# First block's hidden product in whole float32, and another order of the start, in an attention and feed-forward kernel on one NeuronCore

## The chip, the cores and the metric

The kernel runs on one core of a Trainium2 chip. The core has five engines, each with its own instruction queue that is worked off in order: TensorE (PE, matrix products; its weight loads are listed apart as PEld), VectorE (DVE), ScalarE (ACT), GpSimd (POOL) and SyncE (SP). SP and POOL issue the DMA transfers here. The metric is the device time of one execution in microseconds (us).

## The reference, cut to what matters

Inputs are `q`, `k`, `v` of 8 batches, 8 heads, 576 tokens, 64 channels in float32, and two weight matrices in float64, `w_in` (512 x 2048) and `w_out` (2048 x 512).

```
q_d, k_d, v_d = means over 4 neighbouring tokens                 # 144 tokens
out = repeat(softmax(q_d k_d^T / 8) v_d, 4)  +  softmax(q k^T / 8, only |i-j| < 4) v
x = out as (8*576) x 512                                         # tokens x (head, channel)
h = x @ w_in
P = a0 + a1 h + a2 h^2 + a3 h^3 ;  Q = 1 + |b0||h| + |b1| h^2
result = (P / (Q + 1e-6)) @ w_out
```

## The kernel before, in words

The work is written as tasks with an engine, an estimated length, tiles read and written, and sometimes a due time. A planner (`Plan.run`, L117) lists them: on each engine, of the tasks whose inputs are ready, the one with the earliest latest start goes first. The result is a fixed order for each engine; on the chip only the order holds, and each instruction waits for its own inputs. `due_h(n)` (L645) gives the due time of step n of the feed-forward part: `H0` + 8.0 n in the first block, then 6.2 a step.

Attention goes by batches, two heads (a pair) at a time, four pairs a batch. For a pair, `load_qk` and `load_vw` bring the inputs; `scores` (L391) puts a mask into two PSUM banks with two bf16 products (L397) and adds local scores in windows of 64 x 64 (L406); `pool_qk` and `scores_pooled` (L423) do the pooled ones; `softmax_local` and `softmax_pooled` take maxima on DVE and exponentials on ACT (L453, L479); `normalize` scales on DVE; `turned` transposes on PE (L527, L534) and copies back on ACT (L540, L550); `weighted` (L556) multiplies by v (L576, L565), and `put_x` (L608) adds the parts into x on DVE. The first batch (L798 on) runs by itself, two pairs at a time, over all eight banks. Later batches share two banks and run beside the feed-forward part.

The feed-forward part takes blocks of 512 tokens (and two blocks of 256), 16 steps each. Step n: `h_part` (L665) multiplies x by 128 columns of `w_in` into one of two banks; `middle` (L691) reads the bank with four activations (L689) and makes the quotient with further work on ACT and DVE; `o_part` (L724), two steps later, multiplies by 128 rows of `w_out` into four banks (L741). After its last step a block is stored. Products run in fp32r, which keeps fewer bits than float32, so each operand is split into a high part (rounded by a cast) and a low part (the rest), and a product is three: high x high, low x high, high x low. `split_x` (L649) splits x, one ACT cast and one DVE subtraction for each of four 128-column parts.

The weights come as float64. `weights` (L305) loads a chunk of 512 KB into a spot that several chunks share, scales the upper words on ACT (L325), joins the two words into float32 bits on DVE (L328, L331; tile `wb`), casts these to the high part on ACT (L340; `wh`) and subtracts on DVE (L343; `wl`, in the place of `wb`). There are 16 chunks of each matrix. They are wanted in the order in which the first block's steps need them.

Of the kernel before, what the change touches and what calls it, by code (L numbers as in the profile page):

```python
# [9 lines left out]
F32 = mybir.dt.float32  # L10
BF16 = mybir.dt.bfloat16
# [19 lines left out]
NW = 10  # L31
# [136 lines left out]
def attention_moe(  # L168
# [12 lines left out]
    nc = tc.nc  # L181
# [3 lines left out]
    add = plan.add  # L185
# [5 lines left out]
    def put(name, shape, dtype, at=None):  # L191
        nonlocal top
        offset = top if at is None else at
        n = 2 if dtype == BF16 else 4
        for d in shape[1:]:
            n *= d
        if at is None:
            top = -(-(offset + n) // 32) * 32
        ap = nc.alloc_sbuf_tensor_at(name, shape, dtype, offset=offset).ap()
        room = Room(ap, (("S", k) for k in range(offset // 32, -(-(offset + n) // 32))))  # L200
        room.at = offset
        room.size = n
        return room
# [10 lines left out]
    high, low, bits = [], [], [[], []]  # L214
# [9 lines left out]
    xs, xsf = [], []  # L224
# [5 lines left out]
    gb = [put(f"gb{i}", [P, DM], F32, g.at) for i, g in enumerate(gt)]  # L230
    ident = put("ident", [P, P], F32)
    identb = put("identb", [P, P], BF16)
    maskb = put("maskb", [P, NW // 2 * D], BF16)
    cf = put("cf", [P, 8], F32)
    scales = put("scales", [P, 16], F32)
    nms = [put(f"nm{i}", [P, 16], F32) for i in range(4)]
# [54 lines left out]
    add("DVE", 0.1, lambda: nc.vector.memset(scales.ap[:, :NW], scale), (), (scales,))  # L291
    add("DVE", 0.1, lambda: nc.vector.memset(scales.ap[:, NW:], scale / 16.0), (), (scales,))
    add("DVE", 0.2, lambda: nc.vector.tensor_copy(out=identb.ap, in_=ident.ap), (ident,), (identb,))
    add("SP", 0.4, lambda: nc.sync.dma_start(out=maskb.ap, in_=mask), (), (maskb,))

    def setup_coef():
        add("SP", 0.1, lambda: nc.sync.dma_start(out=cf.ap[:, :6], in_=coef), (), (cf,), due=30.0)
# [4 lines left out]
        )  # L302


    def weights(w, f, spot):  # L305
        st = spot.ap.rearrange("p (c f two) -> p c f two", two=2, c=NCC)
        hi, lo, word = high[w][f], low[w][f], bits[w][f]

        def load():
            if w == 0:  # L310
                nc.sync.dma_start(
                    out=st.rearrange("p c f two -> p c (f two)"),
                    in_=w_in[:, 2 * f * P : 2 * (f + 1) * P].rearrange("(c p) f -> p c f", p=P),
                )
            else:
                nc.sync.dma_start(
                    out=st.rearrange("p c f two -> p (c f two)"), in_=w_out[f * P : (f + 1) * P, :]
                )

# [15 lines left out]

        add("SP", 1.4, load, (), (spot,))
        add("ACT", 0.58, scaled, (spot,), (spot,))
        add("DVE", 0.335, upper, (spot,), (lo,))
        add("DVE", 0.6, lower, (spot, lo), (lo,))
        add("ACT", 0.53, lambda: nc.scalar.copy(out=hi.ap, in_=word.ap.bitcast(F32)), (lo,), (hi,))  # L340
        add(
            "DVE", 0.6,
            lambda: nc.vector.tensor_tensor(  # L343
                out=lo.ap, in0=word.ap.bitcast(F32), in1=hi.ap.bitcast(F32), op=ALU.subtract
            ),
            (lo, hi), (lo,),
        )


# [7 lines left out]
        def pos(self, j):  # L357
            return j ^ self.odd

    def load_qk(c):  # L360
        s, b, i = c.slot, c.b, c.i
        add("SP", 1.6, lambda: nc.sync.dma_start(out=s.qk.ap, in_=qk[b, i]), (), (s.qk,))

    def load_vw(c):
        s, b, i = c.slot, c.b, c.i
        add("SP", 0.9, lambda: nc.sync.dma_start(out=s.vw.ap, in_=vw[b, i]), (), (s.vw,))

    def load_pooled(c):

# [21 lines left out]
    def scores(c, bk):  # L391

        s = c.slot

        def issue():
            for j in range(2):
                nc.tensor.matmul(  # L397
                    bk[j].ap[:, : NW // 2 * D], lhsT=identb.ap, rhs=maskb.ap,
                    start=True, stop=False, skip_group_check=True,
                )  # L400
            for w in range(0, NW, 2):
                for j in range(2):
                    js = slice(j * D, (j + 1) * D)
                    for g in range(2):
                        o = (w + g) * WQ
                        nc.tensor.matmul(  # L406
                            bk[j].ap[g * D : (g + 1) * D, w // 2 * D : (w // 2 + 1) * D],
                            lhsT=s.qk.ap[js, 0, PADL + o : PADL + o + D],
                            rhs=s.qk.ap[js, 1, o : o + D],
                            start=False, stop=True, skip_group_check=True,  # L410
                        )

        add("PE", 1.15, issue, (s.qk, identb, maskb), bk)

    def scores_pooled(cs, bk):
        def issue():
# [218 lines left out]
    blocks = block_plan()  # L635
# [29 lines left out]
    def h_part(n, f):  # L665
        k, s = steps[n]
        blk = blocks[k]
        t = blk.t
        ph = hb[n % 2]
        fc = s * blk.fg + f  # L670
        for part_ in range(3):
            i, j = PROD[part_]

            def issue(i=i, j=j, part_=part_):
                for c in range(NCC):
                    nc.tensor.matmul(  # L676
                        ph.ap[:, f * t : (f + 1) * t],
                        lhsT=(high, low)[j][0][fc].ap[:, c, :],
                        rhs=blk.x[i].ap[:, c, :],
                        start=(part_ == 0 and c == 0), stop=(part_ == 2 and c == NCC - 1),  # L680
                    )
# [100 lines left out]


    c0 = [Pair(p) for p in range(NPAIR)]
    due0 = due_h(0) - 6.0
    for c in c0:
        load_qk(c)
    setup_coef()
    add("SP", 0.8, lambda: nc.sync.dma_start(out=vf.ap, in_=vp[0, 0]), (), (vf,))
    for c in c0:  # L790
        load_vw(c)
    for r in range(1, POOL):
        add(
            "POOL", 1.0,
            lambda r=r: nc.gpsimd.dma_start(out=vf.ap, in_=vp[0, r], accum_op=ALU.add),
            (vf,), (vf,), lag=4.0,
        )
    for q in range(2):  # L798
        cs = c0[2 * q : 2 * q + 2]
        for c in cs:  # L800
            pool_qk(c)
        bk = banks
        scores(cs[0], bk[0:2])
        scores(cs[1], bk[2:4])
        scores_pooled(cs, bk[4:6])
        for c, x, y in zip(cs, (bk[0:2], bk[2:4]), bk[4:6]):
            softmax_local(c, x)
            softmax_pooled(c, y)
        for c, x in zip(cs, ((6, 7, 0), (1, 2, 3))):
            normalize(c)  # L810
            turned(c, [bk[i] for i in x])
        weighted(cs, [bk[i] for i in (4, 5, 6, 7)], due0 - 9.0 * (1 - q))
    for w, f, spot in chunks[:9]:
        weights(w, f, spot)
    split_x(0)
    for w, f, spot in chunks[9:]:
        weights(w, f, spot)

    def attend(b):
# [46 lines left out]
    todo = plan.run()  # L866
    ET = mybir.EngineType
    with tc.manual_schedule(engines={getattr(ET, e) for e in ("PE", "DVE", "Activation", "Pool", "SP")}):
        for t in todo:
            t.fn()  # L870


LAG = 2
O_LAG = 2.4
H0 = 45.0
H_FIRST = 8.0
H_STEP = 6.2
SPLIT_EARLY = 6.0
QUAD_GAP = 45.0
EP_DVE = (0,)  # L880


# [60 lines left out]
```

## Time and profile before

| | |
|---|---|
| time, three runs | 997.93, 998.9, 1001.44 us (median 998.9) |
| the profiled execution | 999.81 us, span 998.0 us |
| busy in the span | PE 955.9 (96%), PEld 772.2, DVE 842.2 (84%), ACT 813.9 (82%), POOL 148.2 |
| mean granted clock of PE | 0.973 |
| instructions | 19577 |
| HBM | 72.63 MB read, 9.44 MB written |

A PE record's end is modelled and overlaps the next one, so two starts tell more than a length. The granted clock is a share of 2.4 GHz; 0.50 is 1.2 GHz. One DMA share is the mean of 16 engines. The time outside the span is 1.8 us.

### The profile page before, as it was taken

The numbers are of one execution on the slowest core, as the hardware profiler recorded it, in microseconds if no ns is written. First come the engines' busy times: TensorE is split into PE (matmuls) and PEld (weight loads), VectorE is DVE, ScalarE is ACT, GpSimd is POOL, SyncE is SP. The second block draws the span as 40 slices with busy tenths as digits, with TensorE's granted clock in tenths as the row PEclk, the third lists the DMA queues.
The fourth block names the chain that finished last, engine by engine and source line by source line (L and its number), as shares of the span: only waits on it lengthen the run. The fifth ranks groups of instructions, "written<-read, shape, count | busy, mean of one in ns | idle before, by whom it ended". The sixth has DMA issues, their size and how long they took to land.

```text
span 998.0 us, 19577 instructions
## 1 busy us (share of the span) xinstructions
PE 955.9 (96%) x7264; PEld 772.2 (77%) x7264; DVE 842.2 (84%) x1476; ACT 813.9 (82%) x2082; POOL 148.2 (15%) x177
## 2 busy tenths in 40 slices
PE   3699988999999999999999999999999999999997
PEld 2567766787788878987877887787878878898886
DVE  5889999888788989887888897888888897888886
ACT  5889889886979788778787987888798979867675
POOL 1400212122120303000303030302122220000000
PEclk8589999999999999999999999999999999999999
DMA  9962545422341424102425242433334320100001
GB/s 324 256 239 83 120 134 119 135 45 59 82 128 47 77 70 77 46 22 72 76 67 103 71 92 56 88 101 57 80 69 112 73 52 1 43 1 22 1 1 42
DMA packets 52514, 83.34 MB, mean 84 GB/s; under 512 B 6564, under 2 KB 37284, under 8 KB 52420
## 3 DMA queue, kind: packets, MB, share of 16 engines
q1 hardware_dynamic: 31972, 62.62, 19.0%
q0 software_dynamic: 20448, 19.48, 13.9%
q8 instruction: 57, 0.93, 0.4%
q14 instruction: 37, 0.30, 0.1%
HBM read 72.63 MB, written 9.44 MB: 82 GB/s over the span
## 4 chain that ended last, share of the span: by engine, by line
PE 85%; ACT 6%; DVE 4%; DMA 2%; issue 1%; SPq 0%; ACTq 0%; DVEq 0%
PE psum L741 37%; PE psum L676 37%; PE psum L565 2%; PE psum L406 2%; PE psum L576 2%; ACT m L689 2%; PE psum L527 2%; PE psum L534 1%; PE psum L423 1%; DMA st<-in_w_in_dram 1%; ACT el L453 1%; DMA qk<-in_qk_dram 1%; PE psum L397 1%; ACT gb L689 1%; ACT wh L340 1%
## 5 line engine op out<-in xcount | busy, mean ns | idle before, releaser
L741 PE MATMUL psum<-wh,g 128*128 128x512 f32 x1152 | 366.4, 399 | 2.6 <-DVE g L722 2.3
L676 PE MATMUL psum<-xs,wh 128*128 128x512 f32 (+1 forms) x1280 | 302.2, 375 | 3.1 <-ACT wh L340 1.5
L676 PEld LDWEIGHTS psum<-xs,wh 128*128 128x128 f32 x1280 | 223.9, 190 | 46.5 <-ACT wh L340 2.2
L689 ACT ACTIVATE m<-psum,cf 128x512 f32<-128x512 f32 x288 | 216.9, 757 | 43.2 <-PE psum L676 42.9
L741 PEld LDWEIGHTS psum<-wh,g 128*128 128x128 f32 x1152 | 209.9, 189 | 47.7 <-DVE g L722 2.6
L741 PE MATMUL psum<-wl,g 128*128 128x512 f32 x576 | 224.9, 391 | 0.2 <-DVE wl L343 0.2
L689 ACT ACTIVATE gb<-psum,cf 128x512 f32<-128x512 f32 x144 | 115.7, 803 | 54.9 <-PE psum L741 54.9
L676 PE MATMUL psum<-xs,wl 128*128 128x512 f32 (+1 forms) x640 | 158.7, 370 | 0.0
L376 POOL DMA_DIRECT2D pq<-in_qkp_dram x84 | 73.7, 906 | 485.0 <-DMA pq<-in_qkp_dram 483.8
L713 DVE TENSOR_TENSOR g<-m,m 128x512 fp32r<-128x512 f32 x144 | 99.3, 690 | 45.2 <-ACT m L689 42.2
L704 DVE SCALAR_TENSOR_TENSOR m<-m,cf,m 128x512 f32<-128x512 f32 x144 | 107.4, 746 | 27.5 <-ACT m L689 27.4
L676 PEld LDWEIGHTS psum<-xs,wl 128*128 128x128 f32 x640 | 113.1, 189 | 21.0 <-issue 1.2
L741 PEld LDWEIGHTS psum<-wl,g 128*128 128x128 f32 x576 | 108.4, 188 | 23.9 <-DVE wl L343 0.5
L453 ACT ACTIVATE el<-psum,nm 128x64 f32<-128x64 f32 x320 | 96.9, 348 | 34.1 <-DVE nm L445 34.1
L710 DVE TENSOR_TENSOR m<-m,gb 128x512 f32<-128x512 f32 x144 | 99.3, 690 | 21.2 <-ACT gb L689 16.4
L689 ACT ACTIVATE gb<-m,cf 128x512 f32<-128x512 f32 x144 | 107.1, 744 | 3.6 <-DVE nm L445 3.2
L709 DVE TENSOR_TENSOR m<-m,m 128x512 f32<-128x512 f32 x144 | 98.7, 685 | 8.7 <-ACT m L689 8.7
L716 DVE SCALAR_TENSOR_TENSOR m<-m,g 128x512 f32<-128x512 f32 x144 | 99.4, 690 | 2.9
L721 DVE TENSOR_TENSOR m<-m,m 128x512 f32<-128x512 f32 x144 | 99.4, 690 | 2.9
L722 DVE TENSOR_TENSOR g<-m,m 128x512 fp32r<-128x512 f32 x144 | 98.2, 682 | 0.9
L689 ACT ACTIVATE m<-gb 128x512 f32<-128x512 f32 x144 | 93.6, 650 | 4.9 <-DVE m L709 2.3
L376 POOL DMA_DIRECT2D vp<-in_vp_dram x84 | 72.5, 942 | 160.9 <-DMA vp<-in_vp_dram 153.6
(62 smaller groups left out, 907.0 us busy)
## 6 DMA issues: line engine op xcount, KB each, us to landing
qk<-in_qk_dram SPq DMA_DIRECT2D x32, 590.0 KB, 7.0
pq<-in_qkp_dram POOLq DMA_DIRECT2D x84, 144.0 KB, 3.3
vw<-in_vw_dram SPq DMA_DIRECT2D x32, 320.0 KB, 3.9
out_dram<-xf SPq DMA_DIRECT2D x32, 256.0 KB, 2.0
vp<-in_vp_dram POOLq DMA_DIRECT2D x84, 72.0 KB, 3.1
sl<-in_w_out_dram SPq DMA_DIRECT2D x10, 512.0 KB, 6.8
sl<-in_w_in_dram SPq DMA_DIRECT2D x10, 512.0 KB, 4.8
pq<-in_qkp_dram SPq DMA_DIRECT2D x28, 144.0 KB, 2.1
```

What stands on the lines that cost most here:

```text
L376: lambda d=dst, x=src, r=r: nc.gpsimd.dma_start(out=d.ap, in_=x[b, r, :, i], accum_op=ALU.add),
L453: nc.scalar.activation(out=s.el.ap[:, k, c.pos(j), :], in_=view[:, j, k, :], func=AF.Exp, bias=nm[:, 5 * j + k : 5 * j + k + 1], scale=sca ...
L676: nc.tensor.matmul(ph.ap[:, f * t : (f + 1) * t], lhsT=(high, low)[j][0][fc].ap[:, c, :], rhs=blk.x[i].ap[:, c, :], start=(part_ == 0 and ...
L689: add("ACT", cost, lambda: nc.scalar.activation(out=out_.ap, in_=in_, func=func, **kw), (room_in, cf, *more), (out_,))
L704: lambda: v.scalar_tensor_tensor(out=tb.ap, in0=tq.ap, scalar=b1, in1=tb.ap, op0=ALU.mult, op1=ALU.add),
L709: add("DVE", 0.61, lambda: v.tensor_tensor(out=ta.ap, in0=ta.ap, in1=tq.ap, op=ALU.mult), (ta, tq), (ta,))
L710: add("DVE", 0.61, lambda: v.tensor_tensor(out=ta.ap, in0=ta.ap, in1=u.ap, op=ALU.add), (ta, u), (ta,))
L713: add("DVE", 0.61, lambda: v.tensor_tensor(out=gh.ap, in0=ta.ap, in1=tq.ap, op=ALU.mult), (ta, tq), (gh,))
L716: lambda: v.scalar_tensor_tensor(out=tb.ap, in0=tb.ap, scalar=CONE, in1=gh.ap.bitcast(F32), op0=ALU.add, op1=ALU.mult),
L721: add("DVE", 0.61, lambda: v.tensor_tensor(out=tb.ap, in0=ta.ap, in1=tb.ap, op=ALU.subtract), (ta, tb), (tb,))
L722: add("DVE", 0.61, lambda: v.tensor_tensor(out=gl.ap, in0=tb.ap, in1=tq.ap, op=ALU.mult), (tb, tq), (gl,))
L741: nc.tensor.matmul(ob[sub].ap, lhsT=g[i].ap[:, f0 : f0 + P], rhs=flat((high, low)[j][1][fc].ap), start=(fc == 0 and m == 0), stop=(fc == N ...
```

## The change

- The first block's h product uses float32 operands directly: x as `put_x` left it (`xf`) and the joined bits of `w_in` (`wb`), four products a step in place of twelve; `split_x(0)` is gone. The four products of a step are separate tasks, since each needs only one pair's part of x.
- High and low parts of `w_in` are made by a function of their own, `parts`, after each of the first block's steps, due two units ahead of the same step of the second block. `wl` overwrites `wb`, so it also waits for the first block's product.
- The mask is stored twice over, 128 x 2 x 320, and `scores` puts it in with four products of 64 rows and 64 columns of the array in place of two of the whole array.
- The first batch leaves bank 7 free, and assigns the others anew: scores of all pairs in banks 0 to 3, transposes of three pairs in 6, 4, 5 and of the last in 2, 0, 3. Scores and local softmax of both pairs come ahead of pooling.
- Loads of the first batch and of the first six weight chunks have due times of their own. `H0` is 40 instead of 45.
- `warm`: bf16 products of 128 x 256 into bank 7, whose result nothing reads, are put in front of PE tasks up to the first h product, six tenths of each planned wait long at 0.107 us each (101 of them).

```diff
@@ scores @@
-            for j in range(2):
-                nc.tensor.matmul(
-                    bk[j].ap[:, : NW // 2 * D], lhsT=identb.ap, rhs=maskb.ap,
-                    start=True, stop=False, skip_group_check=True,
-                )
+            for g in range(2):
+                for j in range(2):
+                    js = slice(j * D, (j + 1) * D)
+                    nc.tensor.matmul(
+                        bk[j].ap[g * D : (g + 1) * D, : NW // 2 * D],
+                        lhsT=identb.ap[js, js], rhs=maskb.ap[js, g, :],
+                        start=True, stop=False, skip_group_check=True,
+                    )
@@ weights @@
-        add("ACT", 0.53, lambda: nc.scalar.copy(out=hi.ap, in_=word.ap.bitcast(F32)), (lo,), (hi,))
+        if w:
+            parts(w, f)
+
+    def parts(w, f, due=None):
+        hi, lo, word = high[w][f], low[w][f], bits[w][f]
+        add("ACT", 0.52, lambda: nc.scalar.copy(out=hi.ap, in_=word.ap.bitcast(F32)), (lo,), (hi,), due=due)
...
@@ h_part @@
+        if k == 0:
+            x = xsf[blk.slot][1]
+            for c in range(NCC):
+                def issue(c=c):
+                    nc.tensor.matmul(
+                        ph.ap, lhsT=bits[0][fc].ap[:, c, :].bitcast(F32), rhs=x.ap[:, c, :],
+                        start=(c == 0), stop=(c == NCC - 1),
+                    )
+                add("PE", 0.88, issue, (low[0][fc], part(x, None, 4 * c * t, 4 * t)), (ph,), due=due_h(n) + 0.05 * c)
+            return
@@ first batch @@
-    due0 = due_h(0) - 6.0
+    due0 = due_h(0) - 4.0
+    load_qk(c0[0], -19)
...
+    early = (-18.5, -16, -12, -10, -8, -5)
+    for (w, f, spot), due in zip(chunks[: len(early)], early):
+        weights(w, f, spot, due)
...
-            turned(c, [bk[i] for i in x])
-        weighted(cs, [bk[i] for i in (4, 5, 6, 7)], due0 - 9.0 * (1 - q))
-    for w, f, spot in chunks[:9]:
-        weights(w, f, spot)
-    split_x(0)
+            turned(c, [bk[n] for n in ((6, 4, 5), (6, 4, 5), (6, 4, 5), (2, 0, 3))[2 * q + i]])
+        weighted(cs, [bk[n] for n in ((4, 5, 4, 5), (0, 1, 4, 5))[q]], due0 - 10.0 * (1 - q))
@@ steps @@
                 h_part(n, f)
+                if k == 0:
+                    parts(0, n, due_h(n + blocks[0].nstep) - 2.0)
@@ after planning @@
+    def warm(n):
+        for _ in range(n):
+            nc.tensor.matmul(banks[7].ap[:, : 2 * P], lhsT=identb.ap, rhs=flat(maskb.ap)[:, : 2 * P], start=True, stop=True)
+    pe = [t for t in todo if t.engine == "PE" and t.start < due_h(0) + 5.0]
+    after, end = {}, 3.0
+    for t in pe:
+        n = int(WARM * (t.start - end) / 0.107)
...
-H0 = 45.0
+H0 = 40.0
+WARM = 0.6
```

The order of ACT just ahead of the first activation on a product (`m_166`), before: `sl` and `sx` are weight chunks being scaled, `el` exponentials of the second batch's first pair, `xs` the split of x.

```order
L453 ACTIVATE el_196,sm_187<-psum,nm_183 128x64 x5
L325 ACTIVATE sl_232<-sl_232 128x512
L656 CAST xs_0_152<-xf_1_155 128x512 x2
L453 ACTIVATE el_196,sm_187<-psum,nm_183 128x64 x5
L325 ACTIVATE sl_229<-sl_229 128x512
L325 ACTIVATE sl_231<-sl_231 128x512
L340 CAST wh_5_77<-wb_5_131 128x512
L340 CAST wh_6_78<-wb_6_133 128x512
L689 ACTIVATE m_166<-psum,cf 128x512
```

And now:

```order
L630 ACTIVATE up_191<-psum 128x144
L630 ACTIVATE up_192<-psum 128x144
L325 ACTIVATE sl_230<-sl_230 128x512
L345 CAST wh_11_83<-wb_11_143 128x512
L345 CAST wh_12_84<-wb_12_145 128x512
L325 ACTIVATE sl_232<-sl_232 128x512
L325 ACTIVATE sl_231<-sl_231 128x512
L710 ACTIVATE m_166<-psum,cf 128x512
```

The exponentials of the second batch and the casts of x are gone from this stretch; a third chunk of `w_out` in `sl_230`, one in `sl_232` and two casts of `w_out` chunks 11 and 12 stand there; the chunk of `w_in` in `sl_231` is the last before the activation.

The order of PE at the end of the first batch's attention, before: L565 is the weighted sum of pairs 2 and 3, L676 the first step's products.

```order
L565 MATMUL psum<-et_213,vw_211 64x58 x2
L565 MATMUL psum<-et_220,vw_218 64x58 x2
L676 MATMUL psum<-xs_0_152,wh_0_56 128x512 x4
L676 MATMUL psum<-xs_1_153,wh_0_56 128x512 x4
L676 MATMUL psum<-xs_0_152,wl_0_88 128x512 x4
L676 MATMUL psum<-xs_0_152,wh_1_57 128x512 x4
L676 MATMUL psum<-xs_1_153,wh_1_57 128x512 x4
L676 MATMUL psum<-xs_0_152,wl_1_90 128x512 x4
```

And now, where the first products on pairs 0 and 1 (L685) begin; `ep_215` and `el_212` are pair 2's softmax, L535 and L898 transposes and a filler, L542 further transposes and L584 the pooled weighted sum:

```order
L898 MATMUL psum<-maskb,identb 128x256
L535 MATMUL psum<-ident,ep_215 72x112 x3
L685 MATMUL psum<-xf_1_155,wb_0_89 128x512
L535 MATMUL psum<-ident,ep_215 72x112 x3
L685 MATMUL psum<-xf_1_155,wb_0_89 128x512
L685 MATMUL psum<-xf_1_155,wb_1_91 128x512 x2
L542 MATMUL psum<-ident,el_212 128x128
L584 MATMUL psum<-ept_214,vf 64x144 x4
L584 MATMUL psum<-ept_221,vf 64x144 x4
```

Four float32 products of steps 0 and 1 now stand ahead of the last transposes and the whole weighted sum of pairs 2 and 3; the other four of these steps follow it.

The order of SP at the program's start, before (`qk_193` to `qk_216` belong to pairs 0 to 3, `st` are spots of weight chunks):

```order
L789 DMA vf<-in_vp_dram 72x1024
L362 DMA qk_193<-in_qk_dram 128x1180
L362 DMA qk_200<-in_qk_dram 128x1180
L294 DMA maskb<-in_mask_dram 128x320
L362 DMA qk_209<-in_qk_dram 128x1180
L362 DMA qk_216<-in_qk_dram 128x1180
L366 DMA vw_195<-in_vw_dram 128x640
L366 DMA vw_202<-in_vw_dram 128x640
L297 DMA cf<-in_coef_dram 128x6
L366 DMA vw_211<-in_vw_dram 128x640
L366 DMA vw_218<-in_vw_dram 128x640
L311 DMA st_224<-in_w_in_dram 128x4x256
```

And now:

```order
L294 DMA maskb<-in_mask_dram 128x640
L367 DMA qk_193<-in_qk_dram 128x1180
L311 DMA st_224<-in_w_in_dram 128x4x256
L367 DMA qk_200<-in_qk_dram 128x1180
L311 DMA st_225<-in_w_in_dram 128x4x256
L816 DMA vf<-in_vp_dram 72x1024
L371 DMA vw_195<-in_vw_dram 128x640
L371 DMA vw_202<-in_vw_dram 128x640
L311 DMA st_226<-in_w_in_dram 128x4x256
L367 DMA qk_209<-in_qk_dram 128x1180
L311 DMA st_227<-in_w_in_dram 128x4x256
L367 DMA qk_216<-in_qk_dram 128x1180
```

Weight chunks stand between the pairs' loads; the mask goes first, and pairs 2 and 3 come behind three and four chunks.

## Rows read from the trace of the kernel before

**Rows 1.** Busy us and instructions by engine, granted clock, DMA share and GB/s, by stretch:
```profile
4.00:8.00 4.00, 0.60 (x2) 0.10 (x1) 2.19 (x2) 0.00 (x0) 0.98 (x1) 1.00 1.03 399
8.00:20.00 12.00, 4.74 (x107) 3.62 (x106) 6.55 (x14) 7.54 (x50) 0.83 (x1) 0.84 1.06 331
20.00:40.00 20.00, 15.11 (x222) 11.74 (x224) 15.98 (x36) 16.61 (x66) 7.26 (x9) 0.50 1.04 326
40.00:62.00 22.00, 15.65 (x183) 11.52 (x176) 17.69 (x40) 17.44 (x61) 4.24 (x5) 0.61 0.80 226
...
62.30:188.60 126.30, 115.54 (x845) 88.92 (x844) 119.24 (x221) 110.98 (x283) 20.92 (x24) 0.96 0.48 125
...
188.60:294.20 105.60, 105.60 (x839) 84.69 (x838) 88.98 (x156) 88.02 (x232) 20.64 (x24) 1.00 0.35 80
```

**Rows 2.** Timeline of SP's DMA issues (start, length, instruction), two places:
```profile
53.77 1.37 SPq L311 DMA_DIRECT2D sl<-in_w_in_dram  x2
...
188.64 2.38 SPq L769 DMA_DIRECT2D out_dram<-xf  x4
```

**Rows 3.** Chain of waits up to the first activation (start, length, what):
```profile
3.29 8.84 DMA qk<-in_qk_dram
...
62.21 1.03 ACT wh L340 x2
63.24 1.74 ACT m L689 x3
```

**Rows 4.** Timeline of PE at half clock (to 36) and at full clock:
```profile
8.02 1.35 PE L406 MATMUL psum<-qk 64*64 64x64 f32 x40
...
24.10 1.32 PE L527 MATMUL psum<-ident,ep 112*72 112x112 f32 x6
25.22 1.67 PE L534 MATMUL psum<-ident,el 128*128 128x128 f32 x5
...
31.12 2.19 PE L576 MATMUL psum<-ept,vf 72*64 72x144 f32 x16
33.24 2.40 PE L565 MATMUL psum<-et,vw 64*64 64x58 f32 x80
...
78.42 1.98 PE L676 MATMUL psum<-xs,wh 128*128 128x512 f32 x8
...
81.14 1.98 PE L676 MATMUL psum<-xs,wh 128*128 128x512 f32 x8
...
119.02 1.20 PE L576 MATMUL psum<-ept,vp 72*64 72x144 f32 x16
...
192.59 0.45 PE L397 MATMUL psum<-maskb,identb 128*128 128x320 bf16 x2
192.97 0.81 PE L406 MATMUL psum<-qk 64*64 64x64 f32 x40
```

**Rows 5.** DMA from 0 to 62: all packets, and the largest loads:
```profile
DMA packets 9395, 17.64 MB, mean 284 GB/s; under 512 B 989, under 2 KB 6301, under 8 KB 9389
...
qk<-in_qk_dram SPq DMA_DIRECT2D x7, 590.0 KB, 8.8
```

**Rows 6.** Groups of instructions by line (count, busy us, mean ns of one, idle before):
```profile
L453 ACT ACTIVATE el<-psum,nm 128x64 f32<-128x64 f32 x320 | 96.9, 348 | 34.1 <-DVE nm L445 34.1
...
L343 DVE TENSOR_TENSOR wl<-wb,wh 128x512 fp32r<-128x512 f32 x32 | 21.9, 685 | 1.9 <-ACT wh L340 1.7
...
L576 PE MATMUL psum<-ept,vp 72*64 72x144 f32 x224 | 16.8, 292 | 0.0
```

**Rows 7.** PE busy, granted clock and DMA around a fall and a rise of the clock:
```profile
111.50:112.00 0.50, 0.47 (x4) 0.81 0.84 129
...
115.00:115.50 0.50, 0.50 (x3) 0.78 0.02 2
```

**Rows 8.** Records of L576 under way in stretches of 0.05 us:
```profile
119.05:119.10 0.05, 0.05 (x2) 1.00 0.54 102
...
119.15:119.20 0.05, 0.05 (x4) 1.00 0.40 143
```

More of the change, by code (lines that the diff above doesn't have):

```diff
@@ L232, in attention_moe @@
     identb = put("identb", [P, P], BF16)
-    maskb = put("maskb", [P, NW // 2 * D], BF16)
+    maskb = put("maskb", [P, 2, NW // 2 * D], BF16)
     cf = put("cf", [P, 8], F32)
@@ L293, in attention_moe @@
     add("DVE", 0.2, lambda: nc.vector.tensor_copy(out=identb.ap, in_=ident.ap), (ident,), (identb,))
-    add("SP", 0.4, lambda: nc.sync.dma_start(out=maskb.ap, in_=mask), (), (maskb,))
+    add("SP", 0.4, lambda: nc.sync.dma_start(out=maskb.ap, in_=mask), (), (maskb,), due=-20.0)
     def setup_coef():
@@ L302, in setup_coef, with weights @@
         )
-    def weights(w, f, spot):
+    def weights(w, f, spot, due=None):
         st = spot.ap.rearrange("p (c f two) -> p c f two", two=2, c=NCC)
-        hi, lo, word = high[w][f], low[w][f], bits[w][f]
+        lo, word = low[w][f], bits[w][f]
         def load():
@@ L334, in lower @@
             )
[L336 removed]
+        add("SP", 1.4, load, (), (spot,), due=due)
         add("ACT", 0.58, scaled, (spot,), (spot,))
@@ L345, in weights @@
             ),
-            (lo, hi), (lo,),
+            (lo, hi), (lo,), due=due,
         )
@@ L358, in pos, with load_qk, load_vw @@
             return j ^ self.odd
-    def load_qk(c):
+    def load_qk(c, due=None):
         s, b, i = c.slot, c.b, c.i
-        add("SP", 1.6, lambda: nc.sync.dma_start(out=s.qk.ap, in_=qk[b, i]), (), (s.qk,))
-    def load_vw(c):
+        add("SP", 1.6, lambda: nc.sync.dma_start(out=s.qk.ap, in_=qk[b, i]), (), (s.qk,), due=due)
+    def load_vw(c, due=None):
         s, b, i = c.slot, c.b, c.i
-        add("SP", 0.9, lambda: nc.sync.dma_start(out=s.vw.ap, in_=vw[b, i]), (), (s.vw,))
+        add("SP", 0.9, lambda: nc.sync.dma_start(out=s.vw.ap, in_=vw[b, i]), (), (s.vw,), due=due)
     def load_pooled(c):
@@ L411, in issue @@
                         )
-        add("PE", 1.15, issue, (s.qk, identb, maskb), bk)
+        add("PE", 1.0, issue, (s.qk, identb, maskb), bk)
     def scores_pooled(cs, bk):
@@ L784, in attention_moe @@
     c0 = [Pair(p) for p in range(NPAIR)]
-    due0 = due_h(0) - 6.0
-    for c in c0:
-        load_qk(c)
+    due0 = due_h(0) - 4.0
+    load_qk(c0[0], -19)
+    load_qk(c0[1], -17)
+    load_vw(c0[0], -14)
+    load_vw(c0[1], -13)
+    load_qk(c0[2], -11)
+    load_qk(c0[3], -9)
+    load_vw(c0[2], -7)
+    load_vw(c0[3], -6)
     setup_coef()
-    add("SP", 0.8, lambda: nc.sync.dma_start(out=vf.ap, in_=vp[0, 0]), (), (vf,))
-    for c in c0:
-        load_vw(c)
+    add("SP", 0.8, lambda: nc.sync.dma_start(out=vf.ap, in_=vp[0, 0]), (), (vf,), due=-15)
     for r in range(1, POOL):
@@ L797, in attention_moe @@
         )
+    early = (-18.5, -16, -12, -10, -8, -5)
+    for (w, f, spot), due in zip(chunks[: len(early)], early):
+        weights(w, f, spot, due)
+    bk = banks
     for q in range(2):
         cs = c0[2 * q : 2 * q + 2]
+        for i, c in enumerate(cs):
+            scores(c, bk[2 * i : 2 * i + 2])
+            softmax_local(c, bk[2 * i : 2 * i + 2])
         for c in cs:
             pool_qk(c)
[L802 to L807, printed above, removed]
+        sp = bk[4:6] if q == 0 else bk[0:2]
+        scores_pooled(cs, sp)
+        for c, y in zip(cs, sp):
             softmax_pooled(c, y)
-        for c, x in zip(cs, ((6, 7, 0), (1, 2, 3))):
+        for i, c in enumerate(cs):
             normalize(c)
-            turned(c, [bk[i] for i in x])
-        weighted(cs, [bk[i] for i in (4, 5, 6, 7)], due0 - 9.0 * (1 - q))
-    for w, f, spot in chunks[:9]:
-        weights(w, f, spot)
-    split_x(0)
-    for w, f, spot in chunks[9:]:
+            turned(c, [bk[n] for n in ((6, 4, 5), (6, 4, 5), (6, 4, 5), (2, 0, 3))[2 * q + i]])
+        weighted(cs, [bk[n] for n in ((4, 5, 4, 5), (0, 1, 4, 5))[q]], due0 - 10.0 * (1 - q))
+    for w, f, spot in chunks[len(early) :]:
         weights(w, f, spot)
@@ L866, in attention_moe @@
     todo = plan.run()
+    def warm(n):
[5 more added lines that the diff above has]
+        n = int(WARM * (t.start - end) / 0.107)
+        if n > 0:
+            after[t] = n
+        end = t.end
+        if t.due is not None and t.due == due_h(0):
+            break
     ET = mybir.EngineType
@@ L869, in attention_moe @@
         for t in todo:
+            if t in after:
+                warm(after[t])
             t.fn()
@@ L915 @@
         mask[w % 2, :, w // 2] = np.where(near, 0.0, BIG)
-    mask = mask.reshape(P, NW // 2 * D).astype(ml_dtypes.bfloat16)
+    mask = mask.transpose(1, 0, 2, 3).reshape(1, D, 2, NW // 2 * D).repeat(2, axis=0)
+    mask = mask.reshape(P, 2, NW // 2 * D).astype(ml_dtypes.bfloat16)
     arrays = {
```

## The prediction

> **What bounds the kernel now.** I read the windows by stage first, then the chain of waits around the first activation, the timelines of PE at half and at full clock, and the DMA view of the start. Times are us of one profiled execution, which took 999.81 (span 998.0); the runs shown have a median of 998.9, so 0.9 comes off at the end.
>
> Three stages differ. From 188.6 on PE is busy 105.6 of 105.6, DVE 89.0 and ACT 88.0 [rows 1]: PE bounds, and each us of PE work saved or added there counts in full. The first block runs from the end of its first product (62.3) to its first store at 188.64 [rows 2]: in its 126.3 us DVE is busy 119.2, PE 115.5, ACT 111.0 [rows 1], so DVE leads and PE has some slack. Before that lies the start: the first activation on a product begins at 63.24 [rows 3], with PE at half clock (0.50 from 20 to 40) and the DMA engines full [rows 1]. The clock column reads 1.0 before 16 us, but 40 records of scores take 1.35 at 8.02 against 0.81 at full clock [rows 4]: PE was at 1.2 GHz from the first instruction.
>
> **The start.** The first block's products no longer need `split_x(0)`, scores of pairs 2 and 3 no longer wait for the transposes of pairs 0 and 1, and half of the first two products stands ahead of the last attention work. Three queues can be last at the first activation.
>
> Loads: in after's ACT queue the scaling of `sl_231` still stands before the first activation (the order of ACT in the section on the change), and it is DMA row 35 of SP in both. Summed by size, the transfers up to it are 17.1 MB in both (before: 7 of 590 KB, 6 of 320, 15 of 512, and the small ones, out of 17.64 MB by 62; after has one of 512 more, one of 590 less and 80 KB more mask) [rows 5]. Before issues it in the pair at 53.77 [rows 2], though at 326 GB/s (20 to 40 us [rows 1]) 17.1 MB need 52.5: from 40 to 62 the rate falls to 226, because loads wait for buffers that a late chain frees. With an earlier chain I take 52.5 + 1.5 until data flow + about 1 to land and be scaled = 55. Ends: 45 at the 399 GB/s of 4 to 8 us [rows 1], 62 if it goes as before. The Trainium skill (Perfetto Trace Analysis, Roofline) puts one core's 16 DMA engines at about 435 GB/s; by that the loads would be there at an estimated 41, and something else would be last. The trace differs: 326 is what held for 20 us.
>
> ACT: busy 7.5 + 16.6 + 17.4 = 41.6 up to 62 [rows 1]. After drops ten exponentials of the next batch (0.30 each [rows 6]) and four casts (0.52 [rows 3]) from the queue ahead of the first activation and adds one scaling and one cast (1.1): 37.6. It starts when pair 0 has scores, about 7, so 45 at the earliest, without any wait.
>
> PE: at half clock a pair's transposes take 2.4 (1.1 and 1.3), a pair's scores with their mask 1.6, a weighted sum 4.5 [rows 4]. From the first transposes at about 14.5 after needs 4 x 2.4 + 2 x 1.6 + 2 x 4.5 = 21.8, 60 fillers (an estimate, 256 columns at 1.2 GHz, 0.213 each: 12.8) and eight float32 products (below, 1.71 each: 13.7), 48 in all: 63 without any wait. At full clock it is 24 and hidden. Do the fillers hold the clock? It came back to 1.00 at about 115.1 behind a run of full-width products, yet it stayed at 0.50 through the narrow ones around 31 to 35 and all of 20 to 40 [rows 1, 4, 7]. The fillers are full width but cover six tenths of the planned waits, so I expect a mixture: a third of the way from the loads' 55 to PE's 63, **57.6**, so **-5.6**.
>
> **First block, PE.** A float32 product appears in the trace as two records: the order lists 8 of L576, the trace 16. Records begin two at a time (the two outputs lie on different halves of the partitions) [rows 4, 8]: 8 pairs, 7 gaps, first to last start 1.20 - 0.29 (the mean length of one [rows 6]) = 0.91, so 0.13 for 144 columns, about two cycles a column at 2.4 GHz (0.12). For 512 columns that is 0.43 a record by the cycles, 0.86 a product. If a product took one such slot only, it would be 0.43; I take 0.86, since each product leaves two records. Twelve fp32r products took 2.72 (78.42 to 81.14 [rows 4]), four float32 ones take 3.43: +0.71 a step, over the 15 steps behind the first activation +10.7, less the two products of step 1 that are already done, 1.7: **+8.9** of PE work.
>
> What hides it is the slack: the 126.3 hold 33 half steps of 2.72 (89.8) and one batch of attention, which is 105.5 (188.6 to 294.2, PE without a gap [rows 1]) less 32 x 2.72 = 18.5, of which 1.1 was done before. That leaves 126.3 - 107.2 = 19.1 of idle or half-clock PE time; 10 stay after the change. On DVE the planner's order shows 18 subtractions of low parts in the block instead of 21, 2 of `split_x` instead of 4 and one shift less: 5 x 0.69 + 0.4 = -3.8 [rows 6]. If DVE sets the length, the block takes 122.5; if PE's slack is not used at all, 135.2. Both engines would be above 90% busy, with orders fixed beforehand, so I take a quarter of the way: 125.7, **-0.6**.
>
> **Second block.** Seven low parts and two more subtractions of x move into it: 9 x 0.69 = +6.2 on DVE, which has 16.6 free there [rows 1]; seven casts on ACT, 0.52 each, beside 17.6 free. Cost 0; if PE had to wait for one of them in its order, up to +3.
>
> **The mask.** Two 128x320 products per pair become four of 64 rows and 64 columns of the array. From mask to scores takes 0.375 at full clock [rows 4], of which 2 x 0.133 is columns and 0.11 something else. If four run side by side the columns take 0.133, if none do, 0.53. The scores use the same four quarters: 40 records of 0.053 (64 columns, two cycles each) in 0.81 with the tail, 0.75 without, 2.8 at once. At that rate the mask's columns take 0.19, a gain of 0.08 for each of the 24 pairs behind the first block: **-1.9** (ends -3.2 and +6.4). The Trainium skill (TensorEngine Tiling, Key Properties) says that changing the tiling mode drains the engine; by that the 0.11 only moves from behind the mask to ahead of it and the sum stands, while without such a cost the gain would be 0.08 + 0.11 a pair, 4.6. No row here separates the two.
>
> **Costs at nothing.** SP's order: the six early loads delay pairs 2 and 3 (the fourth `qk` is behind 5.6 MB, about 20 us, against 12.1 before [rows 3]), covered by exponentials of pairs 0 and 1 that keep ACT busy until then; if not covered, it is inside the ends of the start. `maskb` doubled is 80 KB, 0.25. Dropping bank 7 from the first batch costs PE waits there, counted in the mixture.
>
> **Sum.** -5.6 - 0.6 - 1.9 = -8.1: 991.7 in the profiled execution's terms, **991** against the median.
>
> **Rivals.**
> One, the fillers do not hold the clock, and PE's own queue becomes the chain of the start. Then its work alone ends at 63, and PE also idled 4.9 of the 20 us from 20 to 40 for loads and exponentials [rows 1]; with 5 to 7.5 of such waits the first activation comes at 68 to 70.5, +4.8 to +7.3, then -0.6 and -1.9: 1001 to 1004, I say 1003, slower. For it: 20 to 40 at 0.50 in spite of 15.1 of work. Against it: the fillers and the float32 products are full width like those ahead of the rise at 115. It decides once PE's queue ends behind the loads; slower than before from 66 on.
> Two, the first block becomes PE's and none of its slack is used: +8.9 in place of -0.6, with the start as forecast: 1000, no difference. For it: PE's gaps are waits for ACT and DVE, which keep their length. Against it: the new work is independent of both and stands in front of those waits.
> Three, the loads flow as at 4 to 8 us and the clock holds: first activation at 47, -16.2, then as above: 980. For it: spots are asked for earlier. Against: accumulating transfers, which held the rate at 226 to 326.
>
> **Chances.** Forecast 0.53, within 986 to 996; rival one 0.15 (997 to 1006); two 0.20 (997 to 1003); three 0.12 (978 to 986). A difference under 0.3% (996 to 1002) is what a measurement of this kernel cannot tell from none. Faster: 0.50 of the forecast and rival three, 0.62. No difference: 0.03 of the forecast, 0.17 of rival two, 0.05 of rival one, 0.25. Slower: 0.13. The range 983 to 1002 leaves about half of rival three and the upper part of rival one outside.
>
> **What would show it.** Right: first activation at 55 to 60 with the granted clock above 0.6 from 15 to 57, the scaling of `sl_231` among the last waits before it; products of the first block 0.86 apart; its first store near 182 to 184; mask to scores under 0.3; PE without gaps from there on. Wrong: a clock of 0.50 through the start with PE's queue unbroken (rival one), a first block above 133 (rival two), float32 products 0.43 apart, or PE gaps in the second block that end on DVE's low parts.

## The result, and the profile after

The changed kernel took 990.25 us (median of four, 987.5 to 991.5) beside 999.35 of the kernel before: ratio 0.9903, interval 0.9876 to 0.9931, so 9.1 less. It was timed once more with the experiments: 989.9, ratio 0.9890 (0.9872 to 0.9908). The forecast was 991. The profiled execution after is the fastest of its four, 987.5 with a span of 985.7, so its trace holds 12.3 less span than the one before, 3.2 more than the medians allow (2.75 because it lies below its own median, the rest because before's lies above). When the kernel was timed again, the profiled execution (986.77, median 989.9) and one unprofiled (986.83) lay as low; why, no trace shows. Terms read from these two traces may be too large by about 3.

Windows of after, by stage (stretch, length, busy us and instructions of PE, PEld, DVE, ACT, POOL, then granted clock, DMA share, GB/s), against [rows 1]:

```profile
8.00:20.00 12.00, 10.04 (x154) 7.56 (x153) 8.85 (x18) 8.85 (x49) 0.99 (x1) 0.93 1.06 333
20.00:40.00 20.00, 14.66 (x178) 10.78 (x177) 15.32 (x39) 16.16 (x77) 5.32 (x7) 0.93 1.04 317
40.00:59.50 19.50, 14.38 (x194) 8.46 (x193) 13.59 (x28) 12.73 (x26) 6.87 (x8) 0.86 1.03 301
59.50:180.20 120.70, 118.45 (x834) 74.63 (x834) 119.40 (x223) 109.48 (x289) 20.66 (x24) 1.00 0.49 127
180.20:284.80 104.60, 104.60 (x844) 84.00 (x844) 89.18 (x157) 89.00 (x241) 20.63 (x24) 1.00 0.36 81
```

The start has a clock near 0.9 in place of 0.50 to 0.61. In the first block DVE is as busy as before (119.4), but has 1.3 of idle time in place of 7; PE is busy 118.45, idle 2.3, at a granted clock of 1.00 (before 0.96). The second block is PE's without a gap, as before.

The first stores of the first two blocks on SP (start, length), 8.4 and 9.4 earlier than [rows 2] and the 294.15 of before's trace:

```profile
180.23 2.32 SPq L790 DMA_DIRECT2D out_dram<-xf  x4
284.80 2.33 SPq L790 DMA_DIRECT2D out_dram<-xf  x4
```

The chain of waits up to the first activation (start, length, what):

```profile
3.24 9.14 DMA vf<-in_vp_dram
...
12.69 7.79 DMA vf<-in_vp_dram
...
20.78 8.23 DMA vf<-in_vp_dram
...
29.29 7.84 DMA vf<-in_vp_dram
...
37.38 1.20 PE psum L584 x16
...
46.05 6.74 DMA sx<-in_w_out_dram
...
52.87 0.66 ACT sx L325
...
54.74 1.02 DVE xf L616 x4
...
55.81 3.69 PE psum L685 x4
59.49 0.02 issue
59.52 1.84 ACT m L710 x3
```

First come four transfers into `vf` (a load and three that add to it), 7.8 to 9.1 long; each is issued when the one before has landed, so they add up, and the first weighted sum (L584) needs the last. Then ACT waits for a chunk in `sx`, and the copy of the second weighted sum stands behind that scaling, so x is complete late. The first activation is at 59.52 (before 63.24, [rows 3]). ACT's timeline just ahead of it:

```profile
58.55 0.67 ACT L325 ACTIVATE sl<-sl 128x512 f32<-128x512 f32 x1 [1.03 <-DMA sl<-in_w_in_dram]
59.52 0.69 ACT L710 ACTIVATE m<-psum,cf 128x512 f32<-128x512 f32 x1 [0.31 <-PE psum L685]
```

PE's timeline: three float32 products, the last four of steps 0 and 1, and one pair's mask and scores, to be read against [rows 4]:

```profile
45.16 2.75 PE L685 MATMUL psum<-xf,wb 128*128 128x512 f32 x6
...
55.81 5.39 PE L685 MATMUL psum<-xf,wb 128*128 128x512 f32 x8 [3.15 <-DVE xf L616]
...
237.40 0.39 PE L762 MATMUL psum<-wl,g 128*128 128x512 f32 x1
237.72 0.33 PE L404 MATMUL psum<-maskb,identb 64*64 64x320 bf16 x4
237.88 0.75 PE L414 MATMUL psum<-qk 64*64 64x64 f32 x40
238.56 0.74 PE L697 MATMUL psum<-xs,wh 128*128 128x512 f32 x2
```

A product is two records, 0.43 apart. From mask to scores it takes 0.16, before 0.375.

### The profile page after: what moved, and what is told of

The parts are those of the page before. It is cut to its first block, busy times and chain, and to the rows that moved or that the text cites. A ratio compares the mean times of both kernels' runs of the same rounds, so it can differ in the third digit from the quotient of the medians.

```text
span 985.7 us, 19785 instructions
## 1 busy us (share of the span) xinstructions
PE 961.4 (98%) x7365; PEld 758.9 (77%) x7365; DVE 839.4 (85%) x1472; ACT 811.1 (82%) x2078; POOL 148.1 (15%) x177
## 4 chain that ended last, share of the span: by engine, by line
PE 85%; ACT 5%; DVE 4%; DMA 4%; issue 1%; SPq 0%; ACTq 0%; DVEq 0%
PE psum L762 37%; PE psum L697 36%; DMA vf<-in_vp_dram 3%; PE psum L573 2%; ACT m L710 2%; PE psum L584 2%; PE psum L542 2%; PE psum L535 1%; PE psum L414 1%; PE psum L685 1%; PE psum L431 1%; ACT gb L710 1%; DMA sx<-in_w_out_dram 1%; PE psum L404 1%; DVE wl L348 1%
## 5 line engine op out<-in xcount | busy, mean ns | idle before, releaser
L697 PE MATMUL psum<-xs,wh 128*128 128x512 f32 (+1 forms) x1152 | 265.1, 370 | 0.0
L710 ACT ACTIVATE m<-psum,cf 128x512 f32<-128x512 f32 x288 | 219.4, 767 | 39.2 <-PE psum L697 37.5
L697 PEld LDWEIGHTS psum<-xs,wh 128*128 128x128 f32 x1152 | 199.3, 188 | 35.9
L697 PE MATMUL psum<-xs,wl 128*128 128x512 f32 (+1 forms) x576 | 141.6, 368 | 0.0
L697 PEld LDWEIGHTS psum<-xs,wl 128*128 128x128 f32 x576 | 101.3, 189 | 19.0 <-issue 1.2
```

What stands on the lines that cost most here:

```text
L697: nc.tensor.matmul(ph.ap[:, f * t : (f + 1) * t], lhsT=(high, low)[j][0][fc].ap[:, c, :], rhs=blk.x[i].ap[:, c, :], start=(part_ == 0 and ...
L710: add("ACT", cost, lambda: nc.scalar.activation(out=out_.ap, in_=in_, func=func, **kw), (room_in, cf, *more), (out_,))
```

## The experiments

From the profiled execution of each kernel: first activation on a product (F), first store of the first block (S), the stretch between, its granted clock, and the ratio of the times to before's. F of before is read from the chain; its timeline has the record begin at 63.14, so differences to it may be 0.1 too large.

| kernel | F | S | S - F | clock | ratio (interval) |
|---|---|---|---|---|---|
| before | 63.24 | 188.64 | 125.4 | 0.96 | |
| after | 59.52 | 180.23 | 120.7 | 1.00 | 0.9903 (0.9876, 0.9931) |
| after again, a0 | 58.72 | 179.56 | 120.8 | 1.00 | 0.9890 (0.9872, 0.9908) |
| mask alone, m1 | 62.30 | 187.21 | 124.9 | 0.97 | 0.9954 (0.9942, 0.9967) |
| float32 alone, b2 | 60.32 | 182.45 | 122.1 | 0.99 | 0.9952 (0.9937, 0.9968) |
| after without float32, b1 | 60.24 | 187.06 | 126.8 | 0.97 | 0.9965 (0.9951, 0.9979) |
| after without fillers, w0 | 61.35 | 182.73 | 121.4 | 0.99 | 0.9912 (0.9897, 0.9927) |
| more PE work, f1 | 59.64 | 185.81 | 126.2 | 0.99 | 0.9931 (0.9918, 0.9943) |
| more DVE work, d1 | 61.29 | 186.84 | 125.6 | 1.00 | 0.9958 (0.9944, 0.9972) |
| parts due early, p1 | 61.77 | 183.78 | 122.0 | 1.00 | 0.9910 (0.9896, 0.9925) |
| vf earlier, v1 | 57.10 | 179.94 | 122.8 | 0.99 | 0.9899 (0.9884, 0.9914) |
| loads reckoned later, c4 | 55.28 | 180.56 | 125.3 | 0.97 | 0.9906 (0.9887, 0.9925) |
| both, c1 | 51.00 | 173.14 | 122.1 | 0.99 | 0.9824 (0.9805, 0.9842) |
| c1, parts held back, c5 | 51.97 | 174.20 | 122.2 | 1.00 | 0.9838 (0.9815, 0.9861) |

The starts of after, a0, f1 and d1 are the same program, so F varies from 58.7 to 61.3 (a spread of 2.6) without any change.

**Which part of the change pays?** The mask alone in the kernel before (the first diff of the change, and the mask stored twice over):

```
-                nc.tensor.matmul(bk[j].ap[:, : NW // 2 * D], lhsT=identb.ap, rhs=maskb.ap, ...)
+            for g in range(2): ...  # four products of 64 rows and 64 columns
```

> The kernel before with the four-quadrant mask alone. Theory, from the two traces (a batch takes 0.58 less, 0.146 a pair): 24 pairs behind the first block, 3.5, and up to 0.6 in the block and at the start, so 995.3 to 995.8 against 999.35; batches 105.0 to 104.9 us apart instead of 105.5. The prediction's term (0.08 a pair): 997.4. Rival, the whole 0.58 a batch comes from the order around it and not from the mask: 999.3, batches 105.5 apart.

Measured 995.02, 4.6 less by the ratio; from first store to last batch's store 672.7 against before's 676.0, 0.14 for each of 24 pairs. The theory holds, its range missed by 0.3; the prediction's 0.08 a pair was too small.

The float32 product alone, without mask, load order, banks and fillers:

```
+        if k == 0:  # h_part: four float32 products from xf and wb
+                    parts(0, n, due_h(n + blocks[0].nstep) - 2.0)
-    split_x(0)
```

> The kernel before with the float32 product of the first block and the later parts of w_in alone; mask, load order, banks and fillers as before. Theory, without the new order of the start the float32 product gives most of what it gives in the changed kernel (there its removal cost 6.3): first block 119 to 122 instead of 125.4, 993 to 996 against 999.8. Rival, it pays only together with the start's new order, since x is complete late anyway: 998 to 1000. Third, its added PE work of 8.9 counts: 1002 to 1008.

Measured 993.98, ratio 0.9952, 4.8 less: the theory, with a block of 122.1 at its edge. The two alone add to 9.4; the whole change gave 9.7 and 11.0 by its two ratios. So most of the gain needs nothing from the start's new order, and what that order adds is within the intervals. The counter-test, the changed kernel with only the float32 part undone:

```
-        if w:
-            parts(w, f)
+        parts(w, f)
...
-        if k == 0:  # in h_part
+    split_x(0)
```

> The changed kernel with the first block's h product in twelve fp32r products a step again, parts of w_in made at once, x of the first batch split; load order, banks, fillers and mask as changed. Theory, float32 work fills PE's gaps in the first block and so keeps the granted clock at 1.00 there, and the missing split of x shortens the start: without it half-clock stretches come back in the first block (clock 0.96), the block takes 125 instead of 120.7, the first activation comes 1 to 4 later: 996 to 999. Rival, the block gained by other order at its start: 990 to 992, clock 1.00. Third, PE work counts: 8.9 less work shortens the block: 984 to 987.

Measured 996.21, the theory's time and clock; the first activation came only 0.7 later than in after, less than it said. Mask, load order, banks and fillers together (0.9965) are not better than the mask alone (0.9954). The block (windows of all of it and of a part, columns as above) and what PE waited for there (us, times, longest):

```profile
60.24:187.06 126.82, 113.16 (x847) 86.82 (x846) 118.96 (x221) 111.12 (x284) 21.16 (x24) 0.97 0.48 127
...
120.00:140.00 20.00, 16.60 (x104) 12.93 (x105) 19.03 (x35) 12.71 (x26) 5.38 (x6) 0.91 0.45 115
```
```profile
PE psum L683 <- ACT wh L344: 4.0, 3, 2.1
PE psum L748 <- DVE g L729: 2.8, 3, 1.5
PE psum L541 <- ACT ept L547: 2.7, 5, 0.8
```

PE has 5.3 less to do than in after and the block takes 6.1 longer: PE waits 4.0 for the casts that the float32 product does not need, half-clock stretches are back, and DVE idles 7.9. In after PE's longest wait in the block is 0.9, for ACT's `ept`:

```profile
PE psum L542 <- ACT ept L548: 0.9, 1, 0.9
PE psum L535 <- ACT et L559: 0.3, 1, 0.3
```

In before the casts (`wh`) are a small part of PE's waits in the block:

```profile
PE psum L741 <- DVE g L722: 2.3, 3, 1.5
...
PE psum L676 <- ACT wh L340: 1.5, 1, 1.5
```

Of the 10.8 that PE idles there, 1.5 is a direct wait for a cast; the others, for `g` and for attention's tiles, shrank in after too. That they shrank because PE's order no longer hangs on the casts is argued, not shown.

**Do the fillers do anything?** `WARM = 0.0`.

> The changed kernel without the 101 products into bank 7 whose result nothing reads. Theory, the fillers hold the clock through the start: without them the granted clock from 20 to 40 falls to about 0.50 as before, PE's queue takes 3 to 7 longer, first activation at 62 to 66 instead of 59.5, time 993 to 997. Rival, loads and the accumulating transfers set the end of the start: the clock falls but the first activation moves by less than 1, time 990 to 991. Third, the fillers themselves cost PE time: 987 to 989.

Measured 990.22: no difference in time, as the rival said. F came 1.8 later than in after, where the rival said under 1, but equal starts differ by 2.6. Its timeline of PE and its windows:

```profile
5.19 1.34 PE L414 MATMUL psum<-qk 64*64 64x64 f32 x40 [1.66 <-DMA qk<-in_qk_dram]
...
37.78 2.19 PE L584 MATMUL psum<-ept,vf 72*64 72x144 f32 x16 [1.20 <-DMA vf<-in_vp_dram]
...
57.53 6.46 PE L685 MATMUL psum<-xf,wb 128*128 128x512 f32 x8 [2.29 <-DVE xf L616]
```
```profile
8.00:20.00 12.00, 7.17 (x119) 5.13 (x119) 8.99 (x17) 9.20 (x50) 0.98 (x1) 1.00 1.06 341
20.00:40.00 20.00, 11.94 (x113) 8.49 (x113) 14.74 (x32) 16.00 (x75) 5.86 (x7) 1.00 1.04 318
```

By the lengths PE ran at 1.2 GHz until about 40 (2.19 for the weighted sum against 1.20 in after), although the clock column says 1.00. Yet this sum, which waits for `vf`, begins at 37.78, in after at 37.38: up to there PE was not on the path. That the column would read 0.50 was wrong; the engine did run at that speed.

**What bounds the first block afterwards?** Seven float32 products issued twice:

```
+                    if c == 0 and n >= 2 and n % 2 == 0:
+                        nc.tensor.matmul(ph.ap, lhsT=..., rhs=x.ap[:, c, :], start=True, stop=True)
```

> The changed kernel with the first of a step's four float32 products issued twice in steps 2, 4, ... 14 of the first block: 7 more products of 0.86, 6.0 of PE work there (the second starts the sum anew, so the result is the same). Theory, after the change PE has only 2.3 of idle time left in the first block (118.46 busy of 120.71), so the work counts: +3.5 to +6, 994 to 996.5. Rival, the prediction's step that DVE leads and PE's slack hides added PE work: +0 to +1.5, 990 to 991.7.

Seven multiplications on DVE issued twice:

```
+            for _ in range(2 if n in (2, 4, 6, 8, 10, 12, 14) else 1):
                 v.tensor_tensor(out=gh.ap, in0=ta.ap, in1=tq.ap, op=ALU.mult)
```

> The changed kernel with one multiplication of the quotient on DVE issued twice in steps 2, 4, ... 14 of the first block (same operands and result): 7 x 0.69 = 4.8 of DVE work there. Theory, DVE is as full as PE in the first block (119.4 of 120.7 busy): +3 to +5, 993 to 995. Rival, PE alone sets the length: 0 to +1, 990 to 991.

The block's windows of f1 and then of d1:

```profile
59.64:185.81 126.17, 124.61 (x849) 77.85 (x849) 119.73 (x223) 110.78 (x289) 20.88 (x24) 0.99 0.46 121
```
```profile
61.29:186.84 125.55, 120.17 (x834) 74.66 (x833) 123.74 (x229) 110.14 (x289) 20.72 (x24) 1.00 0.47 122
```

In the traces the blocks grow by 5.4 (of 6.0 added) and 4.8 (of 4.8). But after's traces are low ones: beside the blocks of w0 and p1, whose executions lie near the medians (121.4 and 122.0), f1 grows by 4.2 to 4.8 and d1 by 3.5 to 4.2. The medians give +3.1 for f1 (992.98 beside 989.9), below the theory's 3.5, and for d1 994.69, by the ratio to before 5 to 7 more than after. So both engines set the length now, and work added to either shows: from seven tenths to all of it for DVE, from half to nine tenths for PE.

The low parts earlier, `due_h(n + 2)` in place of a block later:

> The changed kernel with the parts of w_in due two steps after their product instead of a block later, so that some 13 more casts of 0.52 (ACT) and subtractions of 0.69 (DVE) lie in the first block and as many fewer in the second: +4 to +9 of DVE work there. Theory, DVE has only 1.3 of idle time left in the first block, so it counts: +3 to +8, 993 to 998. Rival, PE alone sets the length of the block: +0 to +1.5, 990 to 991.7.

Measured 990.8, no clear difference, but the test was void: it moved nothing across the first store. In after all 32 subtractions of low parts lie ahead of that store already, as in p1; inside the block itself the traces have 23 in before, 25 in after and 26 in p1. Groups of DVE from 0 to the store, of after (count, busy, mean ns of one, idle before):

```profile
L348 DVE TENSOR_TENSOR wl<-wb,wh 128x512 fp32r<-128x512 f32 x32 | 21.4, 684 | 0.1
...
L667 DVE TENSOR_TENSOR xs<-xf,xs 128x512 fp32r<-128x512 f32 x4 | 2.8, 688 | 0.1
```

Before has 32 too [rows 6], and eight of `split_x`:

```profile
L659 DVE TENSOR_TENSOR xs<-xf,xs 128x512 fp32r<-128x512 f32 x8 | 5.5, 689 | 0.5 <-ACT xs L656 0.3
```

So "a block later" is a due time that the order hardly follows; DVE lost 2.7 up to its first store, four subtractions of x.

**Is there a better version?** The chain above names two things. `vf` third on SP:

```
-    ... in_=vp[0, 0]), (), (vf,), due=-15)
+    ... in_=vp[0, 0]), (), (vf,), due=-18.8)
```

> The changed kernel with the load of vf third on SP instead of later, so that its three accumulating transfers start about 5 to 8 us earlier. Theory, that chain (four transfers of about 8 each, PE waits for it till 37.4) is last at the first weighted sum and sets the start: first activation 2 to 4 earlier, 986 to 988. Rival, the loads up to sl_231 (scaled at 58.6) set the end of the start: first activation moves by less than 1, 990 to 991.

Measured 989.07 (beside 989.9 and 990.25): not told apart. The first activation came 1.6 to 2.4 earlier, then the loads were last:

```profile
56.53 0.67 ACT L325 ACTIVATE sl<-sl 128x512 f32<-128x512 f32 x1 [2.36 <-DMA sl<-in_w_in_dram]
57.10 0.66 ACT L710 ACTIVATE m<-psum,cf 128x512 f32<-128x512 f32 x1
```

The planner's reckoning of a load, which decides where ACT's scalings stand:

```
-        add("SP", 1.4, load, (), (spot,), due=due)
+        add("SP", 1.7, load, (), (spot,), due=due, lag=4.0)
```

> The changed kernel with the planner's reckoning of a weight load (1.7 and 4.0 instead of 1.4 and 2.0) and vf where the change has it. Theory, ACT's order (copies of the weighted sums ahead of late chunks, the last w_in chunk behind the first activations) is most of the gain, and vf costs 2 to 3 more: 983.5 to 986, first activation 53 to 56. Rival, the chain of accumulating vf transfers, which PE waits for till 37.4, then sets the start alone: first activation 57 or later, 987 to 990.

Measured 989.06: the rival's time, but for another reason. The first activation did come at 55.28; 4.6 came back in the block, whose last part ran partly at half clock (windows, and the weighted sum at 2.19 for 16 records); by the clock of 0.85 over 20.56 that is 3.1 of the 4.6:

```profile
160.00:180.56 20.56, 19.57 (x196) 15.31 (x196) 17.84 (x34) 12.86 (x33) 5.08 (x6) 0.85 0.45 103
```
```profile
160.75 2.19 PE L584 MATMUL psum<-ept,vp 72*64 72x144 f32 x16
```

Both together:

> The changed kernel with vf loaded third and a planner that reckons 1.7 and a delay of 4.0 for a load of weights in place of 1.4 and 2.0: ACT then copies the second weighted sum ahead of a chunk that comes later, and scales the last w_in chunk behind the first activations. Theory, with vf earlier the start waits only for loads that ACT need not wait for: first activation at 54 to 56, and since PE and DVE are both full in the first block (118.5 and 119.4 of 120.7) the gain stays: store at 175 to 178, time 986 to 988.5. Rival, as where vf alone was moved (first activation -2.4, first store -0.3), the work moved out of the start comes back in the block: 989 to 990.5.

Measured 981.74 (980.05 to 984.01), 8.2 less than after beside it and 18 less than before: the version that beats both. ACT's timeline at the start, and the block's window:

```profile
46.22 0.47 ACT L630 ACTIVATE up<-psum 128x144 f32<-128x144 f32 x2
...
50.43 0.68 ACT L325 ACTIVATE sx<-sx 128x512 f32<-128x512 f32 x1 [2.50 <-DMA sx<-in_w_out_dram]
51.00 0.67 ACT L710 ACTIVATE m<-psum,cf 128x512 f32<-128x512 f32 x1
```
```profile
51.00:173.14 122.14, 118.30 (x830) 75.00 (x829) 120.88 (x226) 112.59 (x287) 22.72 (x27) 0.99 0.53 141
```

The copies `up` no longer stand behind a load, and the last `w_in` chunk is scaled behind the first activations; the last wait is still for a load (`sx`, 2.50). First activation 8.5 earlier than in after, store 7.1; both, and the time, lie below what the theory gave (54, 175 and 986). Why c4 and v1 alone kept so little of their earlier start (0 and 0.3 at the store) is shown only for c4, and in part, by the half-clock stretch; that this stretch had to come is not shown.

Last, c1 with the parts of eight chunks really held back until the first store:

```
-                if k == 0:
+                if k == 0 and n < 8:
                     parts(0, n, due_h(n + blocks[0].nstep) - 2.0)
...
+                if k == 0:  # behind store(0)
+                    for m in range(8, 16):
+                        parts(0, m, due_h(m + 16) - 2.0, (part(xs[0][0], None, 0, 4 * DM),))
```

> The kernel with vf third and later-reckoned loads (981.7), with the parts of the last eight w_in chunks held back until the first block's store: all 32 subtractions of low parts lie ahead of the first store in the trace of the changed kernel, so none has really moved a block later. Theory, DVE leads in the first block: six to eight subtractions of 0.69 less there, store 2 to 4 earlier, 978 to 980. Rival, PE is as full (118.3 of 122.1), so the store moves by under 1: 981 to 982.5. Third, the parts come too late for the second block's products: 983 to 985, PE gaps after the store.

```profile
51.97:174.20 122.23, 117.97 (x834) 74.55 (x833) 118.11 (x221) 108.02 (x286) 20.66 (x24) 1.00 0.55 144
```

Measured 981.69, the rival: DVE is relieved of 2.8, and the block stays at 122.2. Yet PE idles 4.3 of it and DVE 4.1, so PE's work alone does not fill it either; what holds the rest is not shown.

## Why the prediction was right, point by point

The time was right, 991 against 990.25, but partly by luck: the sum's terms missed in both directions. From the profiled executions: start -3.7 (predicted -5.6), first block -4.7 (-0.6), second block 104.57 against 105.51 (0 but for the mask, whose four pairs at 0.14 are 0.6 of it), behind the first store -3.9 (-1.9). Start, first block and all that follows (-3.9, the second block among it) add to -12.3; the medians gave -9.1. The first store, at 180.2, came ahead of the 182 to 184 that was to show the forecast right.

**Start.** The place was right: the scaling of `sl_231` was the last ACT work before the activation, and the granted clock was 0.86 to 0.93 from 8 us on, above the 0.6 of the forecast. The first activation came at 59.5 in place of 57.6, and the cause was not the mixture of load volume and PE's queue that I priced. It was the serial chain into `vf`, which the prediction named only as what held the rate down, and ACT's order, with a copy queued behind a load. v1, c4 and c1 show it: with both taken away the activation comes at 51, while the loads flow at 365, 318 and 317 GB/s in c1 (from 8, 20 and 40 us on) against 333, 317 and 301 in after. That the fillers matter was wrong: w0 ran at half clock to 40 and took the same time. Rival one's price (1003) rested on PE's queue with the fillers in it. Where the gain at the start came from is not shown. b2, without `split_x` and with a quarter of the first products early (two of eight ahead of the last weighted sum) but in the old order, gains 2.9; b1, with `split_x` and the new order, gains 3.0; after gains 3.7, and equal starts differ by 2.6.

**First block.** This step failed: "18 subtractions of low parts in the block instead of 21 ... If DVE sets the length, the block takes 122.5", and of that I gave back three quarters for PE's lost slack. First, the order's cut between blocks is not the store: all 32 subtractions precede it in both kernels. Inside the block there are 25 in after against 23 in before, four of x in each, and DVE was as busy as before, 119.4: the 3.8 of relief was not there. Second, the gain was not in DVE's work but in its idle time, 7 to 1.3, and in PE's clock. The float32 product waits for no cast and no split of x, and with it PE's waits are filled; b1 shows the opposite case, with 5.3 less PE work, 7.9 of DVE idle and 6.1 more time. I had kept "orders fixed beforehand" as a reason against using the slack: of the 10 that I expected to stay, 2.3 was left. How much of the 4.7 is the clock (0.96 of 125 is 5.0 lost) and how much the casts is not separated: no run changed one alone. The price of a product, 0.86, was right, and in f1's trace it now counts for the most part.

**Second block.** The cost of 0 was right, but after did not test it: of the seven low parts and two subtractions of x that were to move there none did, and DVE is busy 89.2 as against 89.0. c5 tests it: with the low parts held back, eight subtractions lie in its second block, DVE is busy 91.9, and PE still stays without a gap, 103.71 busy of 103.71.

**Mask.** Right in sign, mis-sized: 0.14 a pair. Mask to scores fell by 0.215: four products together take 0.16, little more than the 0.133 that the prediction priced for one. Ahead of the mask the step from the product before grew from 0.23 to 0.32, and scores to next fell by 0.06. These add to 0.19 at the mask's place; why 0.14 is left over the whole stage is open. The Trainium skill (TensorEngine Tiling, Key Properties), that a change of tiling mode drains the engine, fits the growth of 0.09 ahead; no run separates it.

**Rivals.** Two (PE's +8.9 in full, 1000) did not happen, since the work went into waits; to the next products added it does happen for the most part (f1). Three's 47 was not reached, but its direction was there to be had: c1's 51.

## What to carry to other kernels

An operation that needs fewer prepared operands can cost its engine more and still shorten a stage, when the stage loses its time in waits between engines: count what it no longer waits for, and look at the clock that its gaps cost. When two engines are both nearly full, adding to either shows (f1, d1), while relieving one may give nothing (c5). A load reckoned too short in a fixed order puts finished work behind an unfinished transfer; look at the queue behind each wait on a DMA. Taking away one of two such waits can give nothing in the total (v1, c4), and both together 8 us (c1).

## What the runs showed of the hardware

In w0 the clock column says 1.00 up to 40 us, but 40 score products took 1.34 and a weighted sum 2.19 there (at full clock 0.75 and 1.20): read the lengths of known shapes at a program's start before the column. With fillers, after's scores at 17.82 took 1.01, at 22.23 0.81. A float32 product of 128 x 128 by 128 x 512 leaves two records 0.43 apart at full clock. The load of 288 KB into `vf` and the three transfers that add to it took 7.8 to 9.1 each while loads ran at 317 to 333 GB/s; the smaller adding transfers of later batches (72 and 144 KB) land in 3.2 and 3.3 (medians over the whole execution, by the page).
